# Packed projections, a larger VectorE share of the exponentials, and side work in column strips

## The chip, the cores and the metric

The kernel runs on one core of a Trainium2 chip. A core has TensorE (PE: matrix products, results in PSUM; its weight loads are shown apart as PEld), VectorE (DVE), ScalarE (ACT, activation functions), GpSimd (POOL) and SyncE (SP, whose queue issues most DMAs here). They run side by side, each works through its own instructions in order, and they wait for each other on semaphores. The metric is device time in microseconds (us); lower is better.

## The reference

One transformer block on 2,048 tokens of width 640. Attention has 32 query heads of width 20, and one key and one value head that all of them share.

```python
x = A_x
h = x + _A_ref(_layernorm(x, axis=-1), A_wq, A_wk, A_wv, A_wo)
h2 = h + _B_ref(_layernorm(h, axis=-1), B_w_gate, B_w_up, B_w_down)
...
q = (x @ wq).reshape(B, S, H, Dh).transpose(0, 2, 1, 3)      # H = 32, Dh = 20
scores = jnp.einsum("bhqd,bkd->bhqk", q, x @ wk) * (Dh ** -0.5)
o = jnp.einsum("bhqk,bkd->bhqd", _softmax(scores, axis=-1), x @ wv)
a = o.transpose(0, 2, 1, 3).reshape(B, S, H * Dh) @ wo
...
hid = _gelu(x @ w_gate) * (x @ w_up)                         # 640 -> 1536, tanh form of gelu
b = hid @ w_down                                             # 1536 -> 640
```

## The kernel before

**Tiling.** The tokens make 16 tiles of 128. Heads are padded from 20 to 32 rows, so four heads fill the 128 partitions, and the 32 heads make 8 groups (NG). A pass (t, h) is the attention of tile t's queries for one half of the heads, 4 groups. It consists of 64 blocks: a block is one key tile (16 of them) and one of the four row strips hl, and it gives 128 keys by 512 scores (4 heads by 128 queries). A score block is one matmul with 32 rows (qk_mm, L665); up to four of them run side by side in the four row strips of the array.

**The stream.** Blocks go in cycles of five, three into PSUM banks 0 to 2 and two into banks 3 and 4. ScalarE takes the exponential of three banks or two at once (L743) into pbuf. The sum over keys (PV, L811) then multiplies by v_ext, the values with columns of ones beside them for the softmax's denominator. It uses four column strips of 32, one for each hl, adding into bank 6. In each pass D_UNITS = 12 blocks (D_LAST = 8 in the last tile, none in the first pass) do not go through ScalarE: stream_d lets VectorE turn the scores into the bits of an approximate exponential (L699), with two shifted copies (L708, two blocks at once), and PV adds three weighted terms for each (v_w). Such blocks come only from the last ND_KT = 3 key tiles, and each uses one of PSUM banks 5 and 7, which AUX_pool hands out.

**Side work.** Everything else goes through those same two banks between the cycles: the query projection for the next four tiles (q_proj, L594, copied out by L608), and per tile the output projection (wo_proj, L906, added to the residual by L913), a second layer norm, whose result is transposed by a DMA (L507), gate and up (L942), the gelu (L957, L960 on GpSimd, L963, L969, the tanh L975 on ScalarE), the product hh (L985), and the down projection (L1001, L1009), with the tile's output DMA at L1012. After a pass, normalise transposes the sums (L837), divides and transposes back into onT (L849); Wo begins when both passes of a tile have done so. These matmuls use the whole 128 x 128 array. For gate and up the weights are stationary and the 128 tokens move, so the result has hidden units on partitions, and L985 writes the product into hhT, the form in which the down projection needs it. Wo and down go in column ranges 0 to 512 and 512 to 640.

**The order.** The program first builds a list of tasks with planned durations, dependencies and priorities; _Sched.schedule (L94) runs through it in planned time and fixes each engine's order. The chip then keeps that order, and semaphores hold an instruction until what it needs is there. The planner charges TensorE SWITCH = 0.1 us whenever a task's cfg (row strips "row", column strips "col", whole array None) differs from the one before; it books a DMA on SP as 0.08 us of SP's time, and adds LAG = 0.3 us for side work after its inputs. Where no whole-array task comes for a while it puts in filler matmuls (L1204). PACE_END ends the spacing of side work near the end. The last tile has its own code (last_tile), with the output projection at L1036.

**The start.** GpSimd clears the padding of wq_pad (L449), ScalarE copies the query weights into it (L462), and q_proj_first uses them. GpSimd also takes steps of each layer norm (L483 to L487). The Wo weights are loaded into wo_pad, cleared by L1166. A second, slower form of the kernel follows for inputs whose exponentials would leave the range; it is not entered here.

Of the kernel before, what the change touches and what calls it, by code (L numbers as in the profile page):

```python
# [6 lines left out]
ALU = mybir.AluOpType  # L7
# [17 lines left out]
class _Pool:  # L25
    def __init__(self, n):
        self.free_at = [0.0] * n
        self.users = [[] for _ in range(n)]
        self.busy = [False] * n

# [4 lines left out]
class _Task:  # L35
    __slots__ = ("eng", "fn", "dur", "deps", "prio", "acq", "rel", "dma", "name", "start", "end", "seq",
                 "extra", "sem", "val", "needed", "know", "pos", "lag", "cfg", "after", "paced", "opens", "rides",
                 "groups", "late", "spare")


class _Sched:
# [13 lines left out]
    SPARE_A, SPARE_B = .28, .7  # L55

# [10 lines left out]
    def add(self, eng, fn, dur, deps=(), prio=0.0, acq=(), rel=(), dma=None, name="", lag=0.0,  # L67
# [7 lines left out]
        t.spare = None  # L75
        t.after = list(after)
# [17 lines left out]
    def schedule(self):  # L94
# [28 lines left out]
        while left:  # L123
            best = None
            for e in self.ENGINES:
                cands = []
                for at, t in ready[e]:
# [4 lines left out]
                    for s in t.acq:  # L132
                        p = s.pool
                        open_ = [f for f, b in zip(p.free_at, p.busy) if not b]
                        if not open_:
                            break
# [19 lines left out]
                pick = min((c for c in cands if c[0] <= t0 + 1e-9), key=lambda c: (c[1].prio, c[1].seq))  # L156
# [5 lines left out]
            if e == "pe" and opened is not None and not (t.cfg is None and at - free[e] < self.GAP):  # L162
# [11 lines left out]
            for s in t.acq:  # L174
# [3 lines left out]
                p.busy[i] = True  # L178
                t.extra += p.users[i]
# [9 lines left out]
            else:  # L189
# [16 lines left out]
                if e == "pe" and t.cfg is None:  # L206
                    whole = t.end
                    paced_at = max(paced_at, at) + dur / self.SHARE
# [70 lines left out]
def bass_sequential_preLN__grouped_kv_mqa__glu_gated_geglu__prompt_kernel(  # L279
# [31 lines left out]

    sc = _Sched()
# [10 lines left out]
    wq_pad = sb("wq_pad", [P, ND, H, 32])  # L323
# [3 lines left out]
    wo_pad = sb("wo_pad", [P, NG, D])  # L327
# [32 lines left out]
    ND_KT = 3  # L360
    v_w = sb("v_w", [P, 3, ND_KT, 32])
    wq_sb = dbuf[:].rearrange("p a b n -> p (a b n)")[:, 0:ND * D].rearrange("p (c n) -> p c n", c=ND)
# [23 lines left out]
    AUX, PVB = 5, 6  # L386

# [25 lines left out]
    LAG = 0.3  # L413
    counter = [0.0]
# [34 lines left out]
    z_wq = sc.add("pool", lambda e: e.memset(wq_pad[:, :, :, Dh:32], 0.0), 2.0, prio=nprio(), name="z_wq")  # L449
# [11 lines left out]
    for h in range(2):  # L461
        wq_c.append(sc.add("act", (lambda h: lambda e: e.activation(  # L462
            wq_pad[:, :, 16 * h:16 * h + 16, 0:Dh],
            wq_sb.rearrange("p c (h n) -> p c h n", h=H)[:, :, 16 * h:16 * h + 16, :], ACT.Copy))(h),
            d_act(1600), [dma_wq, z_wq], prio=nprio(), name=f"wqpad{h}"))

    def wq_l(cc, g):
        return wq_pad[:, cc, 4 * g:4 * g + 4, :].rearrange("p a b -> p (a b)")
# [90 lines left out]

    def q_proj_first(h, sl, bk, eng):  # L560
        pr = nprio()

        def part(g0):
            def fn(e):
                ins = None
                for g in range(g0, g0 + 2):
                    for cc in range(ND):
                        ins = e.matmul(bk()[:, g * P:(g + 1) * P], wq_l(cc, 4 * h + g),
# [3 lines left out]
        a = sc.add("pe", part(0), 0.65, ln1_T[0] + [wq_c[h]], prio=pr, acq=[sl], name=f"q0a_{h}")  # L572
        b = sc.add("pe", part(2), 0.65, [a], prio=pr, name=f"q0b_{h}")
        o = qT[:, 0, 4 * h:4 * h + 4, 0:P]

        def ev(e):
            i = bk().rearrange("p (g n) -> p g n", g=4)
            return e.activation(o, i, ACT.Copy) if eng == "act" else e.tensor_copy(o, i)
        q_ready[(0, h)] = [sc.add(eng, ev, d_act(512) if eng == "act" else d_ps(512), [b], prio=pr, rel=[sl],
                                  name=f"q0e_{h}")]  # L580
        xnT_readers[0].append(b)

    last_qk = {}

    def q_proj(c, g, t0, t1):
# [4 lines left out]
        def part(c0, c1):  # L590
            def fn(e):
                ins = None
                for cc in range(c0, c1):
                    ins = e.matmul(bk()[:, 0:n], wq_l(cc, g), xnT[:, cc, t0 * P:t1 * P],  # L594
                                   start=(cc == 0), stop=(cc == ND - 1))
                return ins
            return fn
        deps = [x for t in range(t0, t1) for x in ln1_T[t]] + [wq_c[g // 4]] + xnT_readers[NT - 1][:1]
# [3 lines left out]
        for cc in range(ND):  # L602
            d = sc.add("pe", part(cc, cc + 1), 0.215, deps if d is None else [d], prio=pr, acq=[ax] if d is None else [],
                       lag=0.3, paced=c > 0 and d is None, name=f"q{'abcde'[cc]}_{c}_{g}")
        for t in range(t0, t1):
            xnT_readers[t].append(d)
        o = qT[:, c % 2, g, (t0 % 4) * P:(t0 % 4) * P + n]
# [762 lines left out]
```

## Time and profile before

| | us |
|---|---|
| median of 3 runs (834.09 to 835.84) | 835.21 |
| the profiled execution | 833.07 |
| its span, first to last instruction | 831.0 |
| PE busy | 767.0 (92%) |
| weight loads busy | 303.9 (37%) |
| DVE busy | 648.7 (78%) |
| ACT busy | 799.6 (96%) |
| POOL busy | 92.4 (11%) |
| granted TensorE clock, mean | 0.995 |

Busy time is the time in which an engine has at least one instruction in work. Matmuls are pipelined: one of 512 columns is shown with 0.38 to 0.40 us, and the next can begin 0.22 to 0.23 us after it. The span has three stretches: a start of some 35 us with loads, layer norms and the first projections; the stream; and from about 807 us the last tile's output projection and feed-forward layer.

A row of the costliest groups gives line, engine and operation, result and input, shapes and count; then the busy time and the mean of one in ns; then the idle time of the engine just before such instructions and what ended most of it. A row of the timeline gives start, length, engine, line and shapes. The view of one line gives its shortest, median and longest duration in ns and its first and last start.

### The profile page before, as it was taken

How to read it: one execution, taken by the hardware profiler on the slowest of the kernel's cores; microseconds unless marked ns; L12 is line 12 of the kernel's file. 1: busy time of each engine (PE TensorE's matmuls, PEld its weight loads, DVE VectorE, ACT ScalarE, POOL GpSimd, SP SyncE). 2: the span in 40 equal slices, each digit the busy share in tenths (PEclk: the TensorE clock that was granted, in tenths of full speed). 3: DMA queues.
4: the chain of work that ended last, by engine and by line, in shares of the span. 5: the costliest groups of instructions: out<-in, count | busy, mean ns of one | idle time of the engine just before them, and what ended most of it. 6: DMA issues, size and time to landing. Idle time of an engine off the chain costs nothing.

```text
span 831.0 us, 17917 instructions
## 1 busy us (share of the span) xinstructions
PE 767.0 (92%) x7743; PEld 303.9 (37%) x7800; DVE 648.7 (78%) x1320; ACT 799.6 (96%) x740; POOL 92.4 (11%) x157
## 2 busy tenths in 40 slices
PE   4898999999999999999999999999999999999997
PEld 3322233333234343333323343343434333334345
DVE  7567878888788877987787798878888788777762
ACT  5899999999999999999999999999999999999991
POOL 6500001001001111011000011111101011011010
PEclk9899999999999999999999999999999999999999
DMA  8680000000000000000000000000000000000000
GB/s 215 113 285 1 10 1 9 1 10 9 1 9 10 9 9 2 17 2 17 1 9 10 1 10 9 9 9 10 10 1 17 9 9 2 17 2 9 17 1 20
DMA packets 30347, 18.94 MB, mean 23 GB/s; under 512 B 21944, under 2 KB 28984, under 8 KB 30264
## 3 DMA queue, kind: packets, MB, share of 16 engines
q1 hardware_dynamic: 28808, 17.54, 8.2%
q8 instruction: 62, 1.02, 0.5%
q10 hardware_dynamic: 1456, 0.22, 0.2%
q14 instruction: 21, 0.17, 0.1%
HBM read 10.21 MB, written 2.62 MB: 15 GB/s over the span
## 4 chain that ended last, share of the span: by engine, by line
ACT 85%; PE 9%; DVE 4%; DMA 1%; issue 0%; SPq 0%
ACT pbuf L743 83%; PE ps L665 3%; ACT g_z L975 2%; PE ps L811 2%; PE ps L942 1%; DVE dbuf L699 1%; PE ps L1106 1%; DVE dbuf L708 1%; PE ps L1001 1%; DMA xh<-in_A_x_dram 1%; DVE hhT L985 1%; DMA xnT<-xn_tmp 1%; PE ps L1115 0%; ACT kT L551 0%; PE ps L906 0%
## 5 line engine op out<-in xcount | busy, mean ns | idle before, releaser
L743 ACT ACTIVATE pbuf<-ps 128x1536 bf16<-128x1536 f32 (+1 forms) x674 | 766.8, 1334 | 4.4 <-PE ps L665 4.0
L665 PE MATMUL ps<-qT,kT 32*128 32x512 bf16 x2048 | 289.0, 386 | 38.4 <-ACT pbuf L743 24.8
L699 DVE TENSOR_SCALAR dbuf<-ps 128x512 int16<-128x512 f32 x364 | 247.0, 683 | 88.2 <-PE ps L665 85.8
L811 PE MATMUL ps<-pbuf,v_ext 128*32 128x512 bf16 x1684 | 210.4, 389 | 1.0 <-DVE oT L837 0.5
L811 PE MATMUL ps<-dbuf,v_w 128*32 128x512 bf16 x1092 | 161.2, 380 | 0.0
L665 PEld LDWEIGHTS ps<-qT,kT 32*128 32x128 bf16 x2048 | 73.8, 91 | 226.9 <-ACT pbuf L743 165.7
L708 DVE TENSOR_SCALAR dbuf<-dbuf 128x1024 int16<-128x1024 int16 x364 | 145.2, 433 | 2.7
L960 POOL TENSOR_TENSOR g_z<-g_gs 128x512 bf16<-128x512 bf16 x45 | 49.2, 1092 | 423.6 <-DVE g_gs L957 423.6
L942 PE MATMUL ps<-xnT,wg_sb 128*128 128x128 bf16 x900 | 69.6, 220 | 2.6 <-DVE dbuf L699 1.8
L811 PEld LDWEIGHTS ps<-pbuf,v_ext 128*32 128x32 bf16 x1684 | 40.6, 93 | 82.8 <-issue 68.1
L942 PE MATMUL ps<-xnT,wu_sb 128*128 128x128 bf16 x900 | 69.6, 220 | 0.8 <-DVE dbuf L699 0.4
L1001 PE MATMUL ps<-wd_sb,hhT 128*128 128x128 bf16 (+1 forms) x335 | 62.8, 296 | 2.4 <-issue 1.4
L942 PEld LDWEIGHTS ps<-xnT,wg_sb 128*128 128x128 bf16 x900 | 50.8, 98 | 35.4 <-issue 21.7
L942 PEld LDWEIGHTS ps<-xnT,wu_sb 128*128 128x128 bf16 x900 | 50.8, 98 | 33.7 <-issue 22.8
L811 PEld LDWEIGHTS ps<-dbuf,v_w 128*32 128x32 bf16 x1092 | 45.7, 96 | 14.1 <-issue 2.5
L594 PE MATMUL ps<-xnT,wq_pad 128*128 128x512 bf16 (+1 forms) x143 | 42.9, 370 | 1.5 <-issue 0.6
L906 PE MATMUL ps<-wo_pad,onT 128*128 128x128 bf16 (+1 forms) x225 | 42.4, 297 | 1.7 <-issue 1.4
L1001 PEld LDWEIGHTS ps<-wd_sb,hhT 128*128 128x128 bf16 x360 | 22.9, 97 | 42.0 <-issue 30.7
L483 POOL CAST lnvb<-mv 128x1 bf16<-128x1 f32 x31 | 6.1, 198 | 270.4 <-DVE mv L481 270.4
L957 DVE CAST g_gs<-ps 128x512 bf16<-128x512 f32 x45 | 30.6, 681 | 7.0 <-PE ps L942 6.6
L963 DVE SCALAR_TENSOR_TENSOR g_z<-g_z,g_gs 128x512 bf16<-128x512 bf16 x45 | 30.6, 680 | 5.5 <-POOL g_z L960 5.5
L969 DVE SCALAR_TENSOR_TENSOR g_us<-ps,g_gs 128x512 bf16<-128x512 f32 x45 | 30.6, 680 | 4.4 <-PE ps L942 4.3
(96 smaller groups left out, 407.8 us busy)
## 6 DMA issues: line engine op xcount, KB each, us to landing
out_dram<-xh SPq DMA_DIRECT2D x15, 160.0 KB, 1.8
xh<-in_A_x_dram SPq DMA_DIRECT2D x3, 640.0 KB, 8.6
wg_sb<-in_B_w_gate_dram SPq DMA_DIRECT2D x1, 1920.0 KB, 7.8
wu_sb<-in_B_w_up_dram SPq DMA_DIRECT2D x1, 1920.0 KB, 12.3
wd_sb<-in_B_w_down_dram SPq DMA_DIRECT2D x1, 1920.0 KB, 19.2
dbuf<-in_A_wq_dram SPq DMA_DIRECT2D x1, 800.0 KB, 5.2
wo_pad<-in_A_wo_dram SPq DMA_DIRECT2D x4, 200.0 KB
xnT<-xn_tmp SPq DMA_TRANSPOSE x30, 2.6
```

The lines of the kernel that those rows point to most:

```text
L594: ins = e.matmul(bk()[:, 0:n], wq_l(cc, g), xnT[:, cc, t0 * P:t1 * P], start=(cc == 0), stop=(cc == ND - 1))
L665: return e.matmul(bk.rearrange("p (g n) -> p g n", g=4), kT4[r, kt * P:(kt + 1) * P], qT[r, (t // 4) % 2, 4 * h:4 * h + 4, (t % 4) * P:(t ...
L699: bits = sc.add("dve", lambda e: e.tensor_scalar(buf(0, w), bk(), D_BIAS, 0.0, ALU.add, ALU.max), 0.61, [qk_t] + wq_c, prio=HOT + 100, rel ...
L708: "dve", lambda e, j=j: e.tensor_scalar(buf(j), buf(0), D_SHIFT[j], None, ALU.add), 0.335,
L743: exps.append(sc.add("act", lambda e, w0=w0, w1=w1: e.activation(pbuf[:, p_sl.index, w0:w1], ps[:, w0:w1], ACT.Exp, scale=EXP_SCALE), (1.3 ...
L811: ins = e.matmul(ps[32 * hl:32 * hl + 32, PVB * 512:(PVB + 1) * 512], v, ap(), start=start, stop=stop, tile_position=(0, 32 * hl))
L906: ins = e.matmul(bk()[:, 0:c1 - c0], onT[:, ont.index, g, :], wo_pad[:, g, c0:c1], start=(g == 0), stop=(g == NG - 1))
L942: ins = e.matmul(bk()[:, f * n:(f + 1) * n], wsb[:, cc, (fc0 + f) * P:(fc0 + f + 1) * P], xnT[:, cc, tok], start=(cc == 0), stop=(cc == ND ...
L957: ge = sc.add("dve", lambda e, gsl=gsl, col=col, bk=bk: e.tensor_copy(g_gs[:, gsl.index, col], bk()), d_ps(512), [gm], prio=EVAC + pr, rel ...
L960: sqt = sc.add("pool", lambda e, gsl=gsl, col=col: e.tensor_tensor(g_z[:, gsl.index, col], g_gs[:, gsl.index, col], g_gs[:, gsl.index, col ...
L963: zt = sc.add("dve", lambda e, gsl=gsl, col=col: e.scalar_tensor_tensor(g_z[:, gsl.index, col], g_z[:, gsl.index, col], GELU_K, g_gs[:, gs ...
L1001: ins = e.matmul(bk()[:, 0:c1 - c0], hhT[:, hh.index, fc, tl], wd_sb[:, fc, c0:c1], start=(fc == 0), stop=(fc == NF - 1))
```

## The change

- **Queries and Wo in five groups.** Rows 20 to 31 of each head's 32-row slot were padding. Now 640 rows lie in five groups of 128 (NC): the heads of groups 5 to 7 are cut into pieces (PIECES) and placed in those rows. wq_pk and wo_pk replace wq_pad and wo_pad. Four GpSimd copies fill the packed rows of wq_pk; groups 5 to 7 also stay unpacked in wq_x (in hhT's space), for the first chunk of tiles. After a packed query projection 16 small DMAs on SP (q_pieces) move the pieces to their places in qT. Before a Wo, 16 small DMAs move the pieces of groups 5 to 7 in onT into the packed rows. The last tile uses the unpacked form, loaded into xnT's space (wo_tail) after the side work of tile 10.
- **Fourteen blocks a pass on VectorE** (ten in the last tile), from the last four key tiles.
- **Column strips.** q_proj, wo_proj, gate and up, and down issue each matmul as four of 32 columns (strips), and carry cfg "col" as PV does. Wo and down go in two halves of 320 columns.
- **Gate and up with the tokens stationary.** The result has tokens on partitions; hh is formed in place in g_us, and one transposing DMA for each tile writes hhT.
- **The planner.** It treats side work in column strips as it did whole-array work for fillers and spacing (t.side), holds a bank for a VectorE block that is due (DUE), and lets PV give way to side work while it is fewer than BACKLOG turns behind.

The core of the diff:

```diff
+    BACKLOG, BEHIND = 5, 1e7
+    DUE = 2
...
+        t.side = eng == "pe" and cfg != "row"
...
+                due = e == "pe" and any(t.due is not None and t.due + self.DUE <= turn and not any(
+                    all(s.pool.busy) and not any(s.pool.side) for s in t.acq) for _, t in ready[e])
...
-                        if not open_:
+                        if not open_ or due and t.due is None and any(b and d for b, d in zip(p.busy, p.side)):
                             break
...
+    PIECES = ((0, 3, 0, 12, 5, 0), (3, 2, 0, 8, 5, 12), (3, 1, 8, 4, 7, 12), (4, 1, 8, 4, 7, 16))
+    def pieces():
+        for c, k, r, n, g, d0 in PIECES:
+            for l in range(4):
+                yield (slice(32 * l + Dh + r, 32 * l + Dh + r + n), slice(c, c + k),
+                       slice(32 * l + d0, 32 * l + d0 + n), slice(g, g + k))
...
-    ND_KT = 3
+    ND_KT = 4
...
+    def strips(e, out, lhsT, rhs, start, stop):
+        ins = None
+        for j in range(4):
+            r = slice(32 * j, 32 * j + 32)
+            ins = e.matmul(out[r], lhsT[:, r], rhs, start=start, stop=stop, tile_position=(0, 32 * j))
+        return ins
...
+    for c, k, r, n, g, d0 in PIECES:
+        wq_c.append(sc.add("pool", lambda e, c=c, k=k, r=r, n=n, g=g, d0=d0: e.tensor_copy(
+            wq_v[:, :, 4 * c:4 * c + 4 * k, Dh + r:Dh + r + n], wq_n[:, :, 4 * g:4 * g + 4 * k, d0:d0 + n]),
+            0.1 + n * k / 45.0, [dma_wq], prio=nprio(), name=f"wqp{c}_{r}"))
...
-    D_UNITS, D_LAST = 12, 8
+    D_UNITS, D_LAST = 14, 10
...
+        if not last:
+            pv_t.yields = 2 * n
...
     def wo_proj(t, ont):
-        deps0 = [onorm[(t, 0)], onorm[(t, 1)]] + wo_ready
+        pr = nprio()
+        deps0 = [sc.add("sp", lambda e, x=x: e.dma_start(onT[x[0], ont.index, x[1], :], onT[x[2], ont.index, x[3], :]),
+                        2.0, [onorm[(t, 0)], onorm[(t, 1)]], prio=pr, dma=f"d_op{t % 2}", name=f"op{t}") for x in pieces()]
+        deps0 += [onorm[(t, 0)], onorm[(t, 1)]] + wo_ready
...
-                        ins = e.matmul(bk()[:, 0:c1 - c0], onT[:, ont.index, g, :], wo_pad[:, g, c0:c1],
-                                       start=(g == 0), stop=(g == NG - 1))
+                        ins = strips(e, bk()[:, 0:c1 - c0], onT[:, ont.index, g, :], wo_pk[:, g, c0:c1], g == 0,
+                                     g == NC - 1)
...
+                            return strips(e, bk(), xnT[:, cc, tok], wsb[:, cc, fc0 * P:(fc0 + k) * P], cc == 0,
+                                          cc == ND - 1)
...
+            hh_all.append(sc.add("sp", lambda e, gsl=gsl: e.dma_start_transpose(hhT[:, hh.index, :, :], g_us[:, gsl.index, :]),
+                                 6.0, ups + (x_readers if t0 == 0 else []), prio=pr, acq=[hh], rel=[gsl], dma=f"d_h{t0 % 2}", name=f"hT{t0}"))
...
-            for c0, c1 in ((0, 512), (512, D)):
+            for c0, c1 in ((0, D // 2), (D // 2, D)):
...
-            for g in range(NG):
+            for g in range(NC):
                 q_proj(t // 4 + 1, g, t + 4, t + 8)
```

## The prediction

> **What bounds the kernel now.** I read the chain of waits first, then the costliest groups, then the stretch 60 to 800 us.
>
> ```profile
> ACT 85%; PE 9%; DVE 4%; DMA 1%; issue 0%; SPq 0%
> ...
> L743 ACT ACTIVATE pbuf<-ps 128x1536 bf16<-128x1536 f32 (+1 forms) x674 | 766.8, 1334 | 4.4 <-PE ps L665 4.0
> L699 DVE TENSOR_SCALAR dbuf<-ps 128x512 int16<-128x512 f32 x364 | 247.0, 683 | 88.2 <-PE ps L665 85.8
> L708 DVE TENSOR_SCALAR dbuf<-dbuf 128x1024 int16<-128x1024 int16 x364 | 145.2, 433 | 2.7
> ```
>
> ```profile
> 60.00:800.00 740.00, 699.25 (x7073) 268.75 (x7127) 598.00 (x1172) 738.40 (x650) 65.31 (x90) 1.00 0.03 8
> ```
>
> The second fence gives, after the length, the busy time of PE, weight loads, DVE, ACT and POOL, then clock, DMA share and GB/s. ScalarE's exponentials (L743) never pause: 738.40 of 740 us. PE at 699 looks nearly as full; its timeline says what fills it:
>
> ```profile
> 212.15 0.39 PE L665 MATMUL ps<-qT,kT 32*128 32x512 bf16 x4
> 212.47 0.82 PE L1001 MATMUL ps<-wd_sb,hhT 128*128 128x512 bf16 x3
> 213.23 0.39 PE L665 MATMUL ps<-qT,kT 32*128 32x512 bf16 x2
> 213.54 0.40 PE L811 MATMUL ps<-pbuf,v_ext 128*32 128x512 bf16 x4
> 213.77 0.38 PE L811 MATMUL ps<-dbuf,v_w 128*32 128x512 bf16 x2
> ```
>
> Four strips (L811) go as one round of 0.23 us (213.54 to 213.77), as long as one whole 512-column matmul. A score group to something else takes 0.31 to 0.32 (212.15 to 212.47, 213.23 to 213.54) instead of about 0.216: a change of array shape costs 0.10 us. From 100 to 790 us the start times show 1,324 such changes, 132 us. With a round at 0.226, a 128-column matmul at 0.056 and a change at 0.10, PE needs 627 of those 690 us, 91%.
>
> **Fewer exponentials.** From 100 to 790 us a cycle (three and two blocks) lasts 2.266 us on ScalarE, the tanh taken off, so a block is 0.453 us. VectorE's share rises from 29 x 12 + 2 x 8 = 364 blocks to 29 x 14 + 2 x 10 = 426, 62 more. ScalarE loses 62 x 0.453 = **28.1 us**, on the path: 325 cycles instead of 337. That holds only if nothing else starts to stop ScalarE.
>
> **VectorE.** Each of the 62 blocks adds one L699 and one L708 (364 of each for 364 blocks). Back to back they start 0.605 and 0.336 us apart, so 58 us; by their full durations, 69. Nine query copies (L608, three groups in three chunks, 0.675 each) go, -6. VectorE is then busy (598 + 52 to 63) / 712 = 91 to 93% where it was 81%. It hides beside ScalarE, but blocks and side work share two PSUM banks: a gate or up job holds one 4.1 us from first matmul to end of copy, and banks that come free later make PE wait in order. I take 3 us for this (ScalarE idles 1.6 of 740 now, at 81%); bounds 0 and 21, one L699 of 0.683 us late in each of 31 passes.
>
> **TensorE.** Wo per tile: 8 x 0.226 + 8 x 0.056 = 2.26 becomes 10 rounds of 320 columns. No strip round of 320 is in the trace; from below it is the whole 320-column matmul (L1036, eight in 1.09 us, 0.136), from above a 512 round, 0.226. I take 0.14, as strip and whole rounds agree at 512: 1.40. Down: 3.38 becomes 24 x 0.14 = 3.36. Gate and up: 120 x 0.056 = 6.7 becomes 30 x 0.226 = 6.8. Over 15 tiles -13, 0 and +1. Queries: 15 rounds fewer in three chunks, -10. PV has two more strips per added block, 124 / 4 x 0.226 = +7. Twenty-four score groups less, 0.32 each, -8. Side work is now of PV's shape: the 195 changes from PV to side work vanish, -19. Sum -42: PE needs about (627 - 39) / 664 = 89%. None of it is on the path; it pays for VectorE's delays. At 0.226 a round it would be 34 x 0.086 = 2.9 us more a tile, 95%, still under full.
> By the Trainium skill (TensorEngine Tiling (Array Packing), Restrictions) column tiling switches the fast weight load off, which speaks against strips. In the trace a strip's load takes 93 to 96 ns, a whole one 98, both under the round; by the rule the sum would move towards the 0.226 case only if loads came out from under it.
>
> **Small copies on SP's queue.** New per tile: 16 copies for the packed output rows, issued after the second L849 of the tile, and Wo waits for all. SP issues a copy slowly whatever its size:
>
> ```profile
> L1012 SPq DMA_DIRECT2D out_dram<-xh x15: 332/332/387, 168.2 to 812.4; - x15
> ...
> DMA to landing us min/median/max: 1.8/1.8/2.1
> ```
>
> ```profile
> L427 SPq DMA_DIRECT2D wo_pad<-in_A_wo_dram x4: 303/1396/9036, 39.2 to 50.6; - x4
> ```
>
> At 0.34 from issue to issue the sixteenth goes out 5.1 us after L849 and lands at 6.9. The planner in the kernel books 0.08 per issue and 2.0 for landing: 3.2. It fixes PE's order, so Wo may stand up to 3.3 us (6.9 - 3.2, less its lag of 0.3, rounded) too early, with the score groups behind it and ScalarE behind those. Before, Wo begins 0.76 to 7.2 us after the end of L849 (15 tiles), ready after 0.44; the rest is waiting for a bank. If those waits stay, what is left of 3.3 us adds up to 15.9 us of PE in nine tiles. ScalarE has work for about 0.8 us beyond that (one filled bank group, 0.92, and most of the running one, less the restart of 0.7); taken off each, **9 us** are lost. Bounds: 0 (Wo planned later) and 15 x (3.0 - 0.7) = 34 (each at its earliest).
> By the Trainium skill (DMA: Bandwidth & Descriptors, Why a DMA increments its semaphore by 16 and not by 1) a plain copy before the newest chip costs the sequencer 512 cycles. At 1.2 GHz that is an estimate of 6.8 us for sixteen; the trace's 0.34 decides.
> The 48 query copies have a chunk of slack: nothing. The hidden activations now go through one transposing DMA of 1,536 columns per tile. Before, 640 columns take 1.2 us to issue and 2.6 to land; scaled by 2.4 at most 6.2, at least 4.3 (issue scaled, the rest kept). The planner books 6.0 plus lag: nothing, unless it stands behind the sixteen, some 5.4 of 46 us, about two tiles; within the 34. The hh products lose strided output, 0.05 us x 45, off path.
>
> **Start.** Four GpSimd copies (1,200 elements a partition) come between the query weights' landing (6.39) and the first projection (10.00). By the memset (L449, 1.70 us for 1,920) they take 1.1 us, by L960 (1.04 for 512) 2.4, by L1177 (0.46 for 96) up to 3.7. The first projection has 3.6 us of cover; the layer norms' GpSimd steps, next at 6.74, stand behind them, and VectorE is full from 14 to 32. I take 1 us, bounds 0 and 3. ScalarE's three weight copies hold as many elements as its two. Loss of the 4.4 us memset (L1166) is hidden, as are the 20 Wo loads (6.8 us of SP, first use past 79). **End.** The last tile uses unpacked weights, loaded after tile 10's side work, so its 24 us stay. Tile 14's down projections run at 804 to 812 already; copies and transpose put 7 to 13 us ahead of them and most fits in the last tile's gaps: 1 us, bounds 0 and 5.
>
> **Sum.** -28.1 + 3 + 9 + 1 + 1 = -14.1. The profiled execution took 833.07 (span 831.0 and 2.1 around it), so 819.0; it ran 2.1 below the median 835.21, on which the forecast is **821.1**.
>
> **Rivals.** (1) Nearly all the gain arrives: Wo waits long enough for its bank, no stalls. For: in six of fifteen tiles Wo began over 3.7 us after L849. Against: in seven under 2.3. 835.2 - 28.1 = 807; with 1 us at the start, 808. (2) The two banks and VectorE become the bound: an L699 late in every other pass, 11 us, with the 9, 1 and 1 left: 835.2 - 28.1 + 22 = 829. For: 91 to 93%; against: 89% of PE leaves room. (3) Slower: the issue time on SP. Wo is the hottest side work, and with PE freed it may be placed at its earliest in every tile: 34 us lost, and the other 5 stay: 835.2 - 28.1 + 39 = 846. It decides from 28 / 15 = 1.9 us of ScalarE per tile. (4) The clock falls because little whole-array work is left. The trace speaks against it: 74.40 to 77.82 has no whole matmul at all, and the clock stays:
>
> ```profile
> 74.40:77.82 3.42, 2.83 (x29) 0.71 (x27) 3.41 (x8) 3.42 (x4) 0.00 (x0) 1.00 0.00 0
> 77.82:81.23 3.41, 3.25 (x28) 1.00 (x30) 3.41 (x9) 3.41 (x4) 0.00 (x0) 1.00 0.00 0
> ```
>
> It fell to 0.50 only at 19.74, after 3.4 us with PE 64% busy. Were it to fall for half of the 712 us, PE's 89% would double there: over 1,000.
>
> **Chances.** Forecast (811 to 828) 0.47, rival 1 0.22, rival 2 0.13, rival 3 0.15, rival 4 0.01; 0.02 for no gain, the copies' loss near 28. What a measurement of this kernel tells from no change is 0.2%, 1.7 us. Forecast, rival 1 and most of rival 2 are faster: 0.80; same 0.04; slower 0.16. Range 805 to 840: below, rival 1 with little to spare; above, part of rival 3.
>
> **What would show it.** Cycles of 2.27 us, 325 of them, bear out the first step. PE waits of 1 to 3 us at the Wo line behind a DMA, once a tile, show the queue; none shows rival 1. PE changes near 1,100 from 100 us on, VectorE over 90%. Exponentials waiting for PE with DVE named behind it show rival 2. The forecast is wrong if ScalarE idles over 25 us in mid-kernel or strip rounds of 320 take over 0.2.

## The result and the profile after

The changed kernel took 944.28 us (median of 4 runs, 941.66 to 949.35) beside 834.65 for the kernel before: ratio 1.132, 95% interval [1.127, 1.137]. The forecast of 821.1 was wrong in sign.

The profiled execution took 944.92 (span 943.0); the granted clock fell from 0.995 to 0.922 on average. The exponentials are now L816, scores L734, PV L884, VectorE's bits L772, the two shifted copies L781, the second transpose L925, all strips of side work L422, and the sixteen small copies before Wo L973. First the chain of waits and the costliest groups of the page, after:

```profile
PE 38%; ACT 21%; DVE 21%; SPq 14%; DMA 3%; issue 2%; POOL 0%
...
L816 ACT ACTIVATE pbuf<-ps 128x1536 bf16<-128x1536 f32 (+1 forms) x649 | 746.6, 1293 | 132.5 <-PE ps L734 130.7
L772 DVE TENSOR_SCALAR dbuf<-ps 128x512 int16<-128x512 f32 x426 | 285.8, 681 | 126.2 <-PE ps L734 124.0
...
L422 PE MATMUL ps<-wo_pk,onT 128*32 128x320 bf16 x600 | 47.8, 416 | 95.5 <-DMA onT<-onT 88.4
```

ScalarE was 85% of the chain before and is 21% now: it no longer sets the end. It stood idle 130.7 us for TensorE's scores (4.0 before), and TensorE stood idle 88.4 us at Wo for the small copies, a wait that was not there. The waits view has that one as fourteen times, at most 8.2 us; the fifteenth, 7.1 us in the first tile, is without a named releaser. The third row of groups carries the whole answer; the timeline shows one of the fourteen, here SP, TensorE and ScalarE around the end of tile 2's second pass. Columns: start, length, engine, line, shapes, count, and in brackets the idle time before it.

```profile
193.61 9.96 SPq L973 DMA_DIRECT2D onT<-onT  x15
...
199.64 0.59 PE L884 MATMUL ps<-dbuf,v_w 128*32 128x512 bf16 x4
200.16 0.39 PE L1297 MATMUL ps<-halves,zeros 128*128 128x512 bf16 x1
204.74 2.06 PE L422 MATMUL ps<-wo_pk,onT 128*32 128x320 bf16 x28 [4.19 <-DMA onT<-onT]
206.73 0.61 PE L734 MATMUL ps<-qT,kT 32*128 32x512 bf16 x3
...
199.57 2.44 ACT L816 ACTIVATE pbuf<-ps 128x1536 bf16<-128x1536 f32 x2
207.39 2.37 ACT L816 ACTIVATE pbuf<-ps 128x1536 bf16<-128x1536 f32 x2 [5.38 <-PE ps L734]
```

SP issues fifteen of the sixteen copies in 9.96 us. TensorE's order has Wo (L422) next at 200.55; it waits until 204.74 for the last copy, and the score group behind it can't pass. ScalarE uses up what it has by 202.01 and restarts at 207.39: 2.73 of its 5.38 us go by until the copy is there, the other 2.65 while Wo's strips and the first scores run. That these take so long is shown by the windows of the same stretch (start and end, length, busy PE, weight loads, DVE, ACT, POOL, then clock, DMA share, GB/s):

```profile
200.00:204.70 4.70, 0.55 (x8) 0.10 (x1) 1.36 (x4) 2.01 (x2) 0.00 (x0) 0.77 0.01 2
204.70:208.10 3.40, 3.36 (x38) 1.40 (x38) 1.42 (x3) 0.71 (x1) 0.00 (x0) 0.50 0.00 0
208.10:211.50 3.40, 3.40 (x27) 0.82 (x24) 2.04 (x4) 1.95 (x3) 0.00 (x0) 0.50 0.00 0
211.50:214.90 3.40, 3.39 (x28) 0.75 (x27) 3.00 (x7) 3.20 (x3) 0.00 (x0) 0.81 0.00 0
214.90:218.30 3.40, 2.82 (x34) 0.95 (x38) 3.37 (x9) 3.40 (x5) 1.41 (x3) 1.00 0.02 5
```

By the 0.77 of the first window and the 0.81 of the fourth, the clock is granted at 0.50 from about 202.5, 2 us into the wait, until about 212.8. So the strips of Wo and the scores behind them take twice as long, and ScalarE is short of work a second time. Such a fall comes with all fifteen waits: it begins 1.1 to 4.8 us after the last matmul, lasts 6.8 to 10.2 us, and 3.1 to 8.5 us of it lie behind the start of Wo.

Counted over the whole stream: before, ScalarE had 2 gaps of more than 0.25 us after the first 40 us, 0.6 us in all; now it has 47, together 125.0. Of these the longest gap of each tile, 3.2 to 8.2 us, makes 96; the rest are shorter ones, most of them close behind it. The last exponential ends at 915.5 instead of 806.7, and the end behind it takes 27.5 us instead of 24.3.

### The profile page after: what moved, and what is told of

Same layout as the page of the kernel before. It is cut to its first block, busy times and chain, and to the rows that moved or that the text cites. A ratio compares the mean times of both kernels' runs of the same rounds, so it can differ in the third digit from the quotient of the medians.

```text
span 943.0 us, 22252 instructions
## 1 busy us (share of the span) xinstructions
PE 803.0 (85%) x9708; PEld 270.4 (29%) x9708; DVE 699.3 (74%) x1435; ACT 780.1 (83%) x716; POOL 97.9 (10%) x165
## 4 chain that ended last, share of the span: by engine, by line
PE 38%; ACT 21%; DVE 21%; SPq 14%; DMA 3%; issue 2%; POOL 0%
ACT pbuf L816 20%; SPq L973 14%; PE ps L422 13%; PE ps L734 12%; PE ps L884 10%; DVE dbuf L772 8%; DVE dbuf L781 4%; DMA onT<-onT 2%; DVE oT L913 1%; DVE g_us L1061 1%; DVE g_gs L1034 1%; DVE onT L925 1%; DVE oN L918 1%; DVE g_us L1047 1%; PE ps L1196 1%
## 5 line engine op out<-in xcount | busy, mean ns | idle before, releaser
L816 ACT ACTIVATE pbuf<-ps 128x1536 bf16<-128x1536 f32 (+1 forms) x649 | 746.6, 1293 | 132.5 <-PE ps L734 130.7
L772 DVE TENSOR_SCALAR dbuf<-ps 128x512 int16<-128x512 f32 x426 | 285.8, 681 | 126.2 <-PE ps L734 124.0
L734 PE MATMUL ps<-qT,kT 32*128 32x512 bf16 x2048 | 303.5, 402 | 23.2 <-ACT pbuf L816 12.6
L884 PE MATMUL ps<-pbuf,v_ext 128*32 128x512 bf16 x1622 | 212.9, 403 | 1.7 <-ACT pbuf L816 0.8
L884 PE MATMUL ps<-dbuf,v_w 128*32 128x512 bf16 x1278 | 179.8, 399 | 1.3 <-DVE oT L913 1.2
L781 DVE TENSOR_SCALAR dbuf<-dbuf 128x1024 int16<-128x1024 int16 x426 | 173.2, 440 | 2.3
L734 PEld LDWEIGHTS ps<-qT,kT 32*128 32x128 bf16 x2048 | 75.7, 91 | 287.5 <-ACT pbuf L816 186.8
L422 PE MATMUL ps<-wo_pk,onT 128*32 128x320 bf16 x600 | 47.8, 416 | 95.5 <-DMA onT<-onT 88.4
L422 PE MATMUL ps<-wu_sb,xnT 128*32 128x512 bf16 x900 | 75.2, 388 | 1.1 <-DVE dbuf L772 0.4
L422 PE MATMUL ps<-wg_sb,xnT 128*32 128x512 bf16 x900 | 74.1, 384 | 0.7 <-DVE dbuf L772 0.4
L422 PE MATMUL ps<-wd_sb,hhT 128*32 128x320 bf16 x1440 | 73.6, 303 | 0.5 <-DVE g_us L1047 0.2
L884 PEld LDWEIGHTS ps<-pbuf,v_ext 128*32 128x32 bf16 x1622 | 44.4, 95 | 74.9 <-issue 59.8
L993 DVE TENSOR_TENSOR xh<-xh,ps 128x320 bf16<-128x320 bf16 x30 | 14.5, 484 | 66.9 <-PE ps L422 66.8
L884 PEld LDWEIGHTS ps<-dbuf,v_w 128*32 128x32 bf16 x1278 | 53.3, 99 | 28.6 <-issue 5.2
L422 PEld LDWEIGHTS ps<-wo_pk,onT 128*32 128x32 bf16 x600 | 16.9, 115 | 124.5 <-issue 118.2
L422 PEld LDWEIGHTS ps<-wd_sb,hhT 128*32 128x32 bf16 x1440 | 34.7, 96 | 29.2 <-issue 16.7
L1061 DVE SCALAR_TENSOR_TENSOR g_us<-g_z,g_us 128x512 bf16<-128x512 bf16 x45 | 32.3, 736 | 0.1
L422 PE MATMUL ps<-xnT,wq_pk 128*32 128x512 bf16 (+1 forms) x400 | 31.3, 369 | 0.4 <-DVE dbuf L772 0.4
## 6 DMA issues: line engine op xcount, KB each, us to landing
wd_sb<-in_B_w_down_dram SPq DMA_DIRECT2D x1, 1920.0 KB, 18.1
```

Of the source, the lines that this page charges most:

```text
L422: ins = e.matmul(out[r], lhsT[:, r], rhs, start=start, stop=stop, tile_position=(0, 32 * j))
L734: return e.matmul(bk.rearrange("p (g n) -> p g n", g=4), kT4[r, kt * P:(kt + 1) * P], qT[r, (t // 4) % 2, 4 * h:4 * h + 4, (t % 4) * P:(t ...
L772: bits = sc.add("dve", lambda e: e.tensor_scalar(buf(0, w), bk(), D_BIAS, 0.0, ALU.add, ALU.max), 0.61, [qk_t] + wq_c, prio=HOT + 100, rel ...
L781: "dve", lambda e, j=j: e.tensor_scalar(buf(j), buf(0), D_SHIFT[j], None, ALU.add), 0.335,
L816: exps.append(sc.add("act", lambda e, w0=w0, w1=w1: e.activation(pbuf[:, p_sl.index, w0:w1], ps[:, w0:w1], ACT.Exp, scale=EXP_SCALE), (1.3 ...
L884: ins = e.matmul(ps[32 * hl:32 * hl + 32, PVB * 512:(PVB + 1) * 512], v, ap(), start=start, stop=stop, tile_position=(0, 32 * hl))
```

## The experiments

The theory: the planner books 0.08 us of SP's time for a small copy that takes 0.68 from issue to issue, so it places Wo too early in TensorE's order (below, the order theory; A in the first expectations). Its rivals: the copies cost the time wherever they are planned, by latency or traffic; strips, or the lack of whole-array work, bring the clock down (C); the two PSUM banks and VectorE can't carry fourteen blocks a pass (B). Times are medians; each set of kernels was run beside the kernel before on the same chip (834.66 to 835.42). "True issue" is the first edit below, on which the later kernels build unless another is named.

### The copies' true issue time in the planner

```diff
-                free[e] = at + 0.08
+                free[e] = at + (0.68 if t.name[:2] == "op" or t.name[-1] == "p" else 0.08)
```

> The changed kernel, with one number altered: the planner books 0.68 us of SP's time for each of the small copies (the mean pitch in the trace of the changed kernel) instead of 0.08. Theory A (the Wo matmuls stand too early in PE's order because the 16 copies take 10.2 us to issue and land 12.0 us after the second L925; PE, then ScalarE, stand still, and the clock falls after it): no wait of Wo for onT beyond 0.5 us, clock above 0.98, 806 to 822 us. Rival B (at fourteen blocks VectorE and the two banks are the bound, and the Wo wait only sits where the time is lost): over 880 us. Rival C (the clock falls because no whole-array side work is left, whether PE waits or not): clock still 0.90 to 0.94, over 900 us.

828.47 us, ratio 0.993 [0.991, 0.995]. One planned number, booked for the output and the query copies alike, takes back 116 us: every copy, strip and block of the change is still there. In the groups view of this run:

```profile
L816 ACT ACTIVATE pbuf<-ps 128x1536 bf16<-128x1536 f32 (+1 forms) x649 | 739.5, 1346 | 14.3 <-PE ps L734 10.3 <-PE ps L884 3.3
...
L422 PE MATMUL ps<-wo_pk,onT 128*32 128x320 bf16 x600 | 33.7, 302 | 0.5 <-DVE xh L993 0.3 <-DVE dbuf L772 0.2
```

Wo waits for no DMA any more (95.5 us of idle time before it became 0.5), and ScalarE's idle time before exponentials fell from 132.5 to 14.3. As causes of the loss the rivals fall. But 828.47 lies above what the order theory gave, so something else keeps part of the gain.

### Wo undone, and the copies alone

Wo back to eight padded groups, with strips but without copies:

```diff
-        deps0 = [sc.add("sp", ...) for x in pieces()]
+        deps0 = []
...
-            for g0 in range(0, NC, step):
+            for g0 in range(0, NG, step):
```

> The changed kernel with Wo alone undone to eight padded groups (still in column strips), so that its 16 copies a tile are gone; everything else stays. Wo then takes 16 rounds of 320 columns instead of 10, 0.8 us more of PE a tile. Theory A: 806 to 822 us and a clock above 0.98, as in the run with the true booking. Rival B: over 880 us. Rival C: clock 0.90 to 0.94, over 900 us.

838.1 us, 1.003 [1.002, 1.004], in none of the three ranges written down. Of the loss of 110 us all but 3 are gone here too, which agrees with the order theory, yet it is no faster than before: the last exponential ends at 792.2, 14.5 us ahead of the kernel before, and 46.3 us stand behind it instead of 24.3. One 6.07 us gap of ScalarE at 104 us shows the same fault in small: the transposing DMA of a layer norm stood behind sixteen query copies on SP (95.2 to 106.1), and TensorE waited 6.37 us for it. So the query copies, which the prediction gave as free, cost where another DMA stands behind them.

The reverse, the kernel before with nothing but sixteen such copies a tile, into an unused tile that Wo waits for:

```diff
-        deps0 = [onorm[(t, 0)], onorm[(t, 1)]] + wo_ready
+        deps0 = [sc.add("sp", lambda e, x=x: e.dma_start(junk[x[0], ont.index, x[1], :], onT[x[2], ont.index, x[3], 0:48]),
+                        2.0, [onorm[(t, 0)], onorm[(t, 1)]], prio=pr, dma=f"d_op{t % 2}", name=f"op{t}") for x in pieces()]
+        deps0 += [onorm[(t, 0)], onorm[(t, 1)]] + wo_ready
```

> The kernel before, plus the same 16 copies a tile, from onT to a spare tile that nobody reads (48 columns each instead of 128), for which Wo waits; booked at 0.08 and 2.0 us as in the change. Theory A: Wo waits until some 12 us after the second L849 of each tile, ScalarE idles about 100 us more, 915 to 960 us, with falls of the clock after the waits. Rivals B and C (twelve blocks and whole-array side work are as before): 833 to 845 us, clock 0.99.

991.21 us, 1.188 [1.182, 1.193], more than expected. Its waits view:

```profile
ACT pbuf L752 <- PE ps L674: 139.8, 64, 8.7
...
PE ps L918 <- DMA junk<-onT: 99.0, 14, 8.3
```

These are the after's two waits in a kernel that otherwise is the one before: fourteen waits of Wo, 99.0 us, and 139.8 us of ScalarE. The copies, planned too short, are enough for the whole loss. It is 156 us here and not 110 mainly because nothing is set against it: in the changed kernel the blocks save some 28 us of exponentials, and the gaps of ScalarE add up to 139 us here and to 125 there.

### What a copy costs to issue

The kernel before with 18 lone copies within SBUF, 48 bytes a partition, over 4 to 128 partitions:

```diff
+    for k, n in enumerate((4, 8, 12, 16, 20, 32, 48, 64, 128)):
+        for i in range(2):
+            probe(k, junk[0:n, 2 * k + i, :], zeros[0:n, 0:24])
```

> The kernel before, plus 18 lone copies of 48 bytes a partition on SP after tile 2's attention, two each from 4, 8, 12, 16, 20, 32, 48, 64 and 128 partitions; only the last output waits for them. If the number of partitions sets the issue time (fewer than 16, or not a multiple of 16, being slow): 0.58 to 0.75 us for 4, 8, 12 and 20, and 0.30 to 0.40 for 16, 32, 48, 64 and 128. If it is that the copies stay inside SBUF, or are small: all of them 0.58 or more.

The view of that line (duration on SP shortest, median, longest in ns):

```profile
L1205 SPq DMA_DIRECT2D junk<-zeros x18: 555/599/762, 177.1 to 188.8; - x18
...
DMA to landing us min/median/max: 1.7/1.8/1.9
```

128 partitions took 0.60 us, 32 took 0.56 to 0.60, 8 took 0.63, 12 and 20 took 0.72 to 0.76. The count of partitions sets little of it. In the same run the 160 KB outputs to HBM kept the 0.33 that the prediction showed:

```profile
L1013 SPq DMA_DIRECT2D out_dram<-xh x15: 332/333/383, 170.1 to 814.3; - x15
```

Nor is it that the copies are small. The changed kernel loads its Wo weights in pieces from HBM into SBUF, eight of them with four partitions and 5 KB, and none of the twenty took more than 0.38:

```profile
L466 SPq DMA_DIRECT2D wo_pk<-in_A_wo_dram x20: 295/298/378, 38.0 to 44.9; - x20
```

Copies with both ends in SBUF took about twice as long to issue as these with one end in HBM. A small copy to HBM was not tried, and what in such a copy takes the time is not shown. By the Trainium skill (DMA: Bandwidth & Descriptors, Why a DMA increments its semaphore by 16 and not by 1) a plain copy before the newest chip costs 512 cycles; at 1.2 GHz that is an estimate of 0.43 us. The measurement lies above it for copies within SBUF and below it for those to HBM.

### Filler ahead of Wo

To see what the clock alone cost: the changed kernel with 24 whole-array matmuls ahead of each Wo, so that TensorE does not stand still.

```diff
+                    for _ in range(24):
+                        ins = e.matmul(bk(), zeros[:], halves[:].unsqueeze(1).to_broadcast([P, 4, P]), start=True, stop=True)
```

> The changed kernel with its booking of 0.08, plus 24 filler matmuls (5.2 us at full clock) ahead of each tile's Wo, so that PE works while it would stand waiting for the copies; the results are overwritten. If the loss is the wait alone, ScalarE starves as before: 935 to 955 us. If the falls of the clock after each wait are a part of their own (125 us of ScalarE's idle time, of which 97 are the longest gap of each tile): the falls go, clock above 0.97, and 20 to 35 us come back, 908 to 925 us.

973.28 us, 1.165 [1.161, 1.170]: both expectations missed. TensorE works in order, so the filler held the scores up by itself; its idle time at Wo fell from 95.5 us (6.4 a tile) to 52.2 (3.5 a tile) and the mean clock rose from 0.922 to 0.952, but ScalarE's idle time before exponentials went from 132.5 to 155.5 us. The clock's share of the loss stays open: the gaps outside each tile's longest one make 125.0 - 96 = 29 us, and the longest ones hold some of it too, as the 2.65 us above.

### Why not 807: blocks, strips, GpSimd's clears

With true issue, the exponentials do end early, at 788.6 instead of 806.7; the end behind them grew from 24.3 to 37.8. Three kernels with true issue change one thing each, a fourth two.

Twelve blocks a pass again:

```diff
-    D_UNITS, D_LAST = 14, 10
+    D_UNITS, D_LAST = 12, 8
```

> The run with the true booking (828.5 us), with twelve blocks a pass on VectorE again (eight in the last tile). If the blocks give what the sum booked (28 us) and the 14 us that the run lies above 814 come from elsewhere: 852 to 860 us. If fourteen blocks leave the side work too little of the two banks, so that it falls behind and is made up after the stream (tile 14's side work ended 80 us after its second L925 there, 53 before the change): the stream ends 28 us later, the stretch behind it shrinks from 38 to 25 to 28 us, 840 to 848 us.

838.46 us (834.35 to 843.92), just under the 840 to 848 written down for side work that falls behind and far under the 852 to 860 of the other story. The last exponential ends at 809.9 and the end takes 27 us. Tile 10's side work, from the end of its second L925 to its last addition, takes 77 us; with fourteen blocks 175. The two blocks a pass are worth 10 us here, of the 28 forecast.

Whole-array matmuls in place of strips:

```diff
-        for j in range(4):
-            r = slice(32 * j, 32 * j + 32)
-            ins = e.matmul(out[r], lhsT[:, r], rhs, start=start, stop=stop, tile_position=(0, 32 * j))
-        return ins
+        return e.matmul(out, lhsT, rhs, start=start, stop=stop)
```

The tasks then carry cfg None again.

> The run with the true booking, with each group of four strips issued as one whole-array matmul of the same operands again (cfg None). If the strips' worth is the saved changes of array shape (some 200 to 400 x 0.10 us of PE), and PE has room: 828 to 845 us with PE's changes back near 1,300. If PE has no room without it: over 850 us. If the strips cost (loads, four times the instructions): under 826 us.

824.77 us, 0.988 [0.985, 0.992], 3.7 us less than with strips. GpSimd's four clears of the tail's Wo rows moved to VectorE:

```diff
-        z = [sc.add("pool", lambda e, c=c: e.memset(wo_tail[:, c, :, :], 0.0), 0.8, free_, ...)
+        z = [sc.add("dve", lambda e, c=c: e.memset(wo_tail[:, c, :, :], 0.0), 0.45, free_, ...)
```

> The run with the true booking, with the four clears of the last tile's Wo weights (L1100) on VectorE instead of GpSimd. If GpSimd's clears hold VectorE up (three L781 took 3.35 us beside them instead of 1.1, and a fall of the clock followed): the gaps of ScalarE near 622 us go and 3 to 8 us come back, 820 to 826 us. If not: 827 to 831 us.

823.0 us, 0.986 [0.983, 0.989], 5.5 us less. The reason stands in the timeline of the true-issue run, VectorE and GpSimd around 620 us:

```profile
619.88 2.84 DVE L781 TENSOR_SCALAR dbuf<-dbuf 128x1024 int16<-128x1024 int16 x2
...
618.43 5.39 POOL L1100 MEMSET xnT<- 128x1280 bf16 x4 [4.56 <-PE ps L422]
```

Two shifted copies (L781) take 2.84 us beside GpSimd's clears; the mean of one in that run is 0.437. TensorE stands idle for 2.4 us (621.0 to 623.4), and a clock fall follows, in the windows of that run:

```profile
619.00:622.80 3.80, 1.89 (x14) 0.50 (x14) 3.80 (x5) 3.67 (x4) 3.80 (x4) 1.00 0.00 0
622.80:636.50 13.70, 13.13 (x73) 2.49 (x73) 9.90 (x21) 8.12 (x7) 2.36 (x4) 0.50 0.36 90
```

By the Trainium skill (SBUF — State Buffer, SBUF: two separate sides) VectorE in its faster modes and GpSimd lock one shared pair of ports for a whole instruction; the 2.84 us agree with that.

That the gain comes from there is seen in the start times of the exponentials. Up to 611 us the kernel with VectorE's clears runs 0.65 us behind the true-issue run, and from 640 us on 5.0 to 6.1 us ahead of it; ScalarE's four gaps between 624 and 637, 5.8 us in all, are gone.

Both edits together:

> The kernel with the copies' true issue time in the planner's order, its side work as whole-array matmuls, and the four clears of the tail's Wo rows on VectorE: both of the single changes that gained (824.77 and 823.0) at once. Adding up: if what each gave back is its own (3.7 us and 5.5 us of 828.47), 819.3, range 817 to 822, last exponential at about 781 to 784 and 35 to 38 us behind it. Rival, the two overlap because both only shorten the backlog of side work in front of the last tile: 822 to 825.

826.66 us, 0.990 [0.989, 0.992]: they don't add, and it is slower than either. Its last exponential ends earliest of all, 779.9, 26.8 us ahead of the kernel before, and 45.4 us stand behind it. From the kernel with VectorE's clears, whole-array work is 3.7 us slower; from true issue it was 3.7 faster. And the clears gain 5.5 in one pair and lose 1.9 in the other: there too the last exponential comes earlier, by 6.0 us, but the end behind it grows by 8.7. An edit also makes the planner lay out the tasks anew, so differences of up to some 5 us between the times of two such kernels can't be put down to the edit by the times alone. Of the strips these pairs show only that they gain nothing to speak of.

This kernel, and those below at 816.88, 813.99, 822.14, 821.33 and 822.45, also make the last tile's second and third product (L1227) wait for the first. What this dependency does by itself was not run.

### The side work that ends last

Blocks given back in part, on the kernel with both edits (without that dependency), first twelve a pass from tile 11 on (eight in the last), then thirteen throughout:

```diff
-        return 0 if (t, h) == (0, 0) else D_UNITS if t < NT - 1 else D_LAST
+        return 0 if (t, h) == (0, 0) else D_UNITS if t < 11 else 12 if t < NT - 1 else 8
```

> The same without VectorE's clears (GpSimd clears), and twelve blocks a pass on VectorE from tile 11 on (eight in the last), fourteen before. It gives 20 exponential blocks back to ScalarE, 20 x 0.453 = 9.1 us. Backlog theory (what stands behind the last exponential is side work that two PSUM banks could not take earlier): the end behind the last exponential falls from 37 us to 25 to 28, so the time is 822 to 826, about that of whole-array alone (824.77) or up to 3 us better. Rival (the end is the latency of the last tiles' chain and doesn't depend on VectorE's blocks): 832 to 835.

> The same with thirteen blocks a pass throughout (nine in the last), GpSimd clears. It gives 32 blocks back, 32 x 0.453 = 14.5 us. Backlog theory: about half of the difference between fourteen and twelve blocks, the end behind the last exponential some 25 to 30 us, time 823 to 830. Rival (the blocks are worth their exponentials in full, the end stays at 37 us): 837 to 840.

825.4 and 828.14 us. The expectations speak of GpSimd's clears, but in both kernels the clears are VectorE's, so they are compared with the 826.66 above and not with 824.77. The first gives back 20 blocks, 9.1 us by their price: the last exponential comes 11.0 us later, the end behind it falls from 45.4 to 32.3, and the time falls by 1.3. Thirteen give back 31 (the expectation has 32), 14.0 us: 12.8 later, 34.5 behind, and 1.5 us more. So what the blocks cost on ScalarE is repaid at the end nearly in full, as the backlog theory has it (what stands behind the last exponential is side work that came late), though the ends are longer than the 25 to 30 us that it gave.

Which resource makes the side work late? On the kernel with VectorE's clears (823.0), first the two GELU products that stand in SBUF alone are cut to 16 of their 512 columns (VectorE relieved), then gate and up add two of five parts of the contraction (TensorE and the banks relieved):

```diff
-                    g_z[:, gsl.index, col], g_z[:, gsl.index, col], GELU_K, g_gs[:, gsl.index, col],
-                    ALU.add, ALU.mult), 0.6, [sqt, ge], ...
+                    g_z[:, gsl.index, j * 512:j * 512 + 16], g_z[:, gsl.index, j * 512:j * 512 + 16], GELU_K,
+                    g_gs[:, gsl.index, j * 512:j * 512 + 16], ALU.add, ALU.mult), 0.08, [sqt, ge], ...
```

> The kernel with the copies' true issue time and VectorE's clears (823.0, last exponential 783.5, 37.2 us behind it), with the two products of GELU that stand only in SBUF done on 16 of their 512 columns (so the output is not the reference's). That takes about 90 x 0.6 = 54 us off VectorE (3.6 us a tile) and leaves how long side work holds its two PSUM banks and TensorE. If VectorE's 90% is what makes the side work late: the end behind the last exponential falls by 8 to 13 us to 24 to 29, time 808 to 814. If the two banks and TensorE's share are: 820 to 823, the end still 35 to 38 us.

```diff
-                    for cc in range(ND):
+                    for cc in (0, ND - 1):
```

> The same kernel with gate and up adding up two of their five parts of the contraction (so the output is not the reference's). That takes 6 x 3 x 0.22 = 4 us a tile off TensorE and off the time for which the two banks are held, and leaves VectorE's work as it is. If the banks and TensorE make the side work late: the end behind the last exponential 24 to 29 us, time 808 to 814. If VectorE does: 820 to 823. If both are short by about the same, each of the two runs gains, 812 to 818.

816.88 us, 0.978 [0.976, 0.979], and 813.99, 0.974 [0.973, 0.976]. Each gains, by 6 and 9 us, both within the 812 to 818 that was written down with the second run for "both are short"; the first run's own two ranges missed 816.88. The stretch 200 to 600 us, in this order: the kernel with VectorE's clears, GELU cut, contraction cut:

```profile
200.00:600.00 400.00, 383.97 (x4826) 124.79 (x4827) 356.11 (x718) 395.35 (x348) 35.52 (x50) 1.00 0.10 19
```

```profile
200.00:600.00 400.00, 387.25 (x4874) 126.71 (x4871) 336.86 (x716) 396.66 (x348) 33.83 (x48) 1.00 0.08 18
```

```profile
200.00:600.00 400.00, 371.97 (x4488) 121.25 (x4484) 361.17 (x729) 396.00 (x348) 37.55 (x50) 0.99 0.10 21
```

VectorE is busy 356 of 400 us (89%) and TensorE 384 (96%). Taking 19 us off the one or 12 off the other lets the side work catch up: tile 10's takes 157 us, then 125 and 83, and the end behind the last exponential 37.2, then 30.9 and 26.6. So neither alone is the bound; of these two cuts the one at TensorE and the banks gained more.

### The best that was found

VectorE's clears and fewer blocks in the late tiles, with strips:

> The kernel at 823.0 (copies' true issue time, strips, VectorE's clears) with twelve blocks a pass from tile 11 on and eight in the last. Whole-array alone went from 824.77 to 825.4 with this, so blocks given back to ScalarE are paid by a shorter end and no more: 821 to 825, last exponential 790 to 793 and 29 to 32 us behind it. If VectorE's clears and the lighter late tiles help one another: 818 to 821.

822.14 us, 0.985 [0.984, 0.986]. The last exponential ends at 793.2, 9.7 us later than in the kernel at 823.0, with 27.1 us behind it, 10.1 less: again the blocks are repaid and no more. Then tile 14's Wo, and in another run tile 13's as well, from the unpacked rows of the last tile, without copies (PLAIN = 14, 13):

```diff
+        plain = t >= PLAIN and "general" not in state
-        deps0 = [sc.add("sp", ...) for x in pieces()]
+        deps0 = [] if plain else [sc.add("sp", ...) for x in pieces()]
...
+                                     wo_tail[:, g // 2, g % 2, c0:c1] if plain else wo_pk[:, g, c0:c1], g == 0, g == ng - 1)
```

> The kernel at 822.14 (copies' true issue time, strips, VectorE's clears, twelve blocks a pass from tile 11 on), with tile 14's Wo taken from the unpacked rows that the last tile uses anyway, so without its sixteen copies; six rounds of 320 more (0.14 us each). If the copies' 12 us of latency in tile 14 hold up the end: its Wo starts 6 to 10 us earlier, and 3 to 6 us of that arrive, 816 to 819. If the backlog of the tiles before it holds up the end: 821 to 824.

> The same for tiles 13 and 14. If the copies' latency holds up the end through both tiles: 814 to 818. If the backlog does: 821 to 824, as before.

821.33 (819.99 to 821.84), ratio 0.984 [0.982, 0.985], and 822.45 us. Without copies the last addition of tile 14's Wo starts 5.3 us after the tile's second transpose instead of 16.5, and the tile's last addition starts 58 instead of 71 us after it, but the end does not move. With twelve late blocks the 26 to 27 us behind the last exponential are near the 24.3 of before. The copies' latency in the last tiles is not what holds them, nor is tile 14: its last addition ends at 803.5 of 819.7 us. What is left is the last tile's own chain; that was not tried.

The kernels side by side, from the profiled execution of each (span and last exponential):

| kernel | time, us | last exponential ends | behind it |
|---|---|---|---|
| before | 834.65 | 806.7 | 24.3 |
| after | 944.28 | 915.5 | 27.5 |
| true issue | 828.47 | 788.6 | 37.8 |
| ... twelve blocks | 838.46 | 809.9 | 26.9 |
| ... whole array | 824.77 | 785.9 | 36.7 |
| ... clears on VectorE | 823.0 | 783.5 | 37.2 |
| ... both | 826.66 | 779.9 | 45.4 |
| ... strips, clears, late twelve | 822.14 | 793.2 | 27.1 |
| ... and tile 14 without copies | 821.33 | 793.3 | 26.4 |

## Why the prediction was wrong

**The step that failed: "Small copies on SP's queue", and in it the size, not the mechanism.** It said that Wo waits for sixteen copies that the planner books too short, with scores behind Wo and ScalarE behind those, and that is what happened. It took 0.34 us from issue to issue from a row of outputs to HBM; the copies took 0.585 (four partitions) to 0.744 (twelve) on average and stood 0.68 apart. So the last copy was issued 10.2 and Wo began 12.0 us after the second transpose, where the step had 5.1 and 6.9. That left Wo not "up to 3.3 us" but 3.9 to 8.2 us early, well past the 0.8 us of work that ScalarE has in hand, in every tile. Nine us of loss were forecast, 34 as the bound; ScalarE idled 125. Two terms were missing beside the pitch: the clock at half speed, 3.1 to 8.5 us of it behind each wait, and that a longer booking error is no longer covered by Wo's waits for its bank, on which the 9 rested. The upper bound was wrong because it kept the same 0.34: a price from a row of another kind of copy belonged in the range with both ends.

**Rival 3** was the right story, given 0.15 and priced at 846. Its turning point, 1.9 us of ScalarE per tile, was passed four times over (125 / 15 = 8.3).

**"Fewer exponentials"** stands. With the copies booked truly and fourteen blocks a pass the last exponential ended 18.1 to 26.8 us earlier, beside 28.1 forecast.

**"VectorE", +3, and "End", +1,** were too small, and at another place. The delay of the banks hardly shows as idle ScalarE (4.7 us in gaps in the kernel at 823.0) but as side work that falls behind: the end behind the last exponential grew by 12.9 us there, above the bound of 5. This is rival 2, which named the two banks, seen at the tail and not in front of exponentials.

**"TensorE"** was right on rounds of 320 columns, 0.136 us as against 0.14 taken, but the strips' other gain mostly failed. The changes from PV to side work did vanish (186 to none from 100 to 780 us, in the kernel at 823.0), but those to and from fillers, which use the whole array, rose from 41 to 158, and all changes of array shape together went only from 1,304 to 1,217. TensorE was 96% busy from 200 to 600 us (95% in the kernel before, by the same measure), and strips bring nothing that the pairs above could tell.

**The transposing DMA** took 1.44 us to issue and landed after 3.6 to 5.4, mostly below the estimate of 4.3 to 6.2 (median 3.8), and no wait came of it. The query copies were not quite free, as the 6.07 us gap shows. **"Start"** held: the first exponential began at 15.1 instead of 14.6, and the four copies together took 1.9 us (scaled plainly, the row of L1177 gives 5.75 and not the 3.7 written there). **Rival 4** fell: with strips nearly throughout, the clock was 0.994 on average once Wo no longer waited; it fell behind waits, not for lack of whole-array work.

The forecast's number, 821.1, is close to the best kernels above (821.33 to 823.0), but mending the planned duration alone gave 828.47; the rest took VectorE's clears and later edits. The terms are others too: less lost in the stream, more at the end. That is agreement by chance in the sum.

## What to carry to other kernels

Where a planner fixes an in-order engine's sequence, price every new kind of instruction from a row of exactly that kind (here SBUF to SBUF, not SBUF to HBM) before trusting the order, and ask of each wait put ahead of a busy engine what queues behind it: 0.6 us wrong on each of sixteen small copies a tile cost 116 us. Work taken off the bounding engine must be found a place to finish: follow the backlog of the side work from tile to tile, not only the idle time of the bounding engine. Whether few large copies would serve a hot task better was not tried; leaving them out and keeping the padding (838.1) was not faster than planning them truly (828.47).

## What the runs showed of the hardware

- A lone copy within SBUF held SP's queue 0.56 to 0.76 us over 4 to 128 partitions, while one of 160 KB to HBM held it 0.33 and small loads of 5 KB from HBM 0.30; landing took 1.8 us for the copies within SBUF and for those to HBM.
- In the fifteen waits of 3.9 to 8.2 us without matmuls TensorE's clock fell to 0.50 between 1.1 and 4.8 us after the last matmul and came back 3.1 to 8.5 us after matmuls had begun again, 6.8 to 10.2 us in all; once it stayed at 0.50 for 13.7 us after an idle gap of only 2.4 us (TensorE busy 1.89 of 3.80 us). By the Trainium skill (TensorE: Matmul & The Clock Gate, What's actually happening) an idle window of about 3.4 us halves the clock and a busy one of that length restores it. The trace agrees on the half; the fall also came after shorter gaps, as the 2.4 us show, and recovery took about one to two and a half such lengths behind the waits and nearly four in that one case.
- Two of VectorE's shifted copies took 2.84 us instead of 0.87 while GpSimd cleared memory, and moving the clears to VectorE took that stretch's 5.8 us of ScalarE's gaps away.
